# Low parts by negative copies and accumulating transfers, and a negated sine taken into a product

## The chip, the cores and the metric

The kernel runs on one core of a Trainium2 chip. The core has a matrix engine (TensorE: PE for its matmuls, PEld for its weight loads) and three engines for element-wise work (VectorE: DVE, ScalarE: ACT, GpSimd: POOL); SyncE (SP) only issues transfers. Each engine takes its instructions in the order in which they were written to its queue. Transfers (DMA) are issued from the queues of SP, ACT and POOL. The metric is the device time of one execution in microseconds.

## The reference

The input u has 2048 tokens of 448 features. It is normalised over its features (xn), and the output is the sum of three terms:

```
xn  = layernorm(u)
out = u + ssm(xn) + glu(xn)

ssm:  dt = exp(log_dt);  A = -exp(log_A_real) + i*A_imag;  C = (C_real + i*C_imag)*dt
      K[d,l] = 2 * Re( sum over n of C[d,n] * exp(A[d,n]*dt[d]*l) )      # 448 x 2048, n = 0..255
      y = causal convolution of xn with K, by an FFT of length 4096;  y + xn * D_skip
glu:  h = sigmoid(xn @ w_gate) * (xn @ w_up)       # 448 -> 1792
      h @ w_down                                    # 1792 -> 448
```

Everything is float32.

## The kernel before, in words

Two Python generators write the program, and a loop at the end of the kernel takes the next piece from the one that is further behind by its planned cost (`done`, `total`). `conv()` writes the state-space part: loads, normalisation and preparation of the parameters (`prep`), then `kgen`, which computes the kernel K in 56 chunks of 8 features, then `spectra`, which does the products in the frequency domain and the way back. `glu()` writes the gated unit. A planner that simulates the engines then sets the order of the instructions on each queue; `tc.high_priority(HP)` moves an instruction ahead in it and `tc.issue_after` holds one behind another.

**The gated unit.** The 1792 hidden features are taken as 14 tiles of 128 (`f`), in five weight groups of 3, 3, 3, 3 and 2 tiles; the tokens are taken in two halves of 1024, each in two blocks (`t`) of 512. A matmul takes float32r operands, which keep fewer bits than float32, so each operand is held as a high part (a copy rounded to float32r) and a low part (what the rounding left), and three products are summed. High and low parts are:

- weights of the gate and up projections: `wh`, `wl` (128x1024), from the loaded tile `wraw`, of which there is one buffer; `wh` is a cast on ACT (L758) and `wl` is a subtraction on DVE (L762, for f = 0 L760);
- weights of the down projection: `dh` by a cast on ACT (L788), `dl` (128x448) by a subtraction on POOL (L789), from the loaded tile `rd`;
- the gated activations of a block: `hf` (128x512, one buffer) is made on DVE from PSUM (L718); `hh` is its cast on ACT (L723), `hl` a subtraction on DVE (L725).

A call of `gate` is one tile f for one block of tokens: two series of 11 matmuls (L707), the first half for the gate and the second for the up projection. A weight step is two such calls. At the end of a weight group come the down projections (L819), four of 128 tokens for each block, each a series of three matmuls (`dh,hh`, `dl,hh`, `dh,hl`) per weight tile, summed into `acc` on DVE (L824). In the first half of the tokens all 14 weight tiles are split as told; those of the first group and of two tiles of the second are loaded and split again on POOL in the second half (L769, L770, L796), the other nine are stored to DRAM by SP (L779) and loaded from there (L774, L800).

**The chunks.** For each chunk, two matmuls give phases in PSUM (L534), ACT turns them into sines and cosines in the tile `S` (L542 to L545), DVE multiplies them with magnitudes `me` and `mf` into `Et` and `Ft` (L599 to L601), and PE takes those in 64 small matmuls (L615). The magnitudes are products on POOL (L500, L512), made for two chunks at a time with two buffers, with two squarings on ACT (L525). `S` has five slots of 512 values: sine, cosine, minus sine (half of it used), cosine, sine, with one ACT pass each for the absolute values (L542), the sines (L543), the minus sines (L544) and the cosines (L545). L599 multiplies one half of `me` with cosine and sine; L600 multiplies the other with cosine and minus sine, read backwards; L601 makes `Ft`. The phases for a pair of chunks are loaded by SP (L484).

Of the kernel before, what the change touches and what calls it, by code (L numbers as in the profile page):

```python
# [21 lines left out]
N = 256  # L22
# [4 lines left out]
TWO_PI = 2.0 * math.pi  # L27
# [8 lines left out]
HELD = 9  # L36
LATE = 3.6
# [11 lines left out]
DC = 8  # L49
# [81 lines left out]
def s4d_glu_kernel(ctx, tc, io):  # L131
# [322 lines left out]
    def kgen(pk):  # L454
# [5 lines left out]
            ("S1", [128, 5, 2 * DC, 32], F32), ("Et1", [128, 2, 2 * DC, 64], F32),  # L460
            ("Et0", [128, 2, 2 * DC, 64], F32), ("Ft", [128, 2, 2 * DC, 32], F32),
            ("S0", [128, 5, 2 * DC, 32], F32), ("mf0", [128, 4 * DC, 32], F32),
            ("me0", [128, 4 * DC, 64], F32), ("pm0", [128, 12, NCH * 2 * DC], F32),
            ("ph0", [128, 2, N], F32R), ("ph1", [128, 2, N], F32R),
        ]
        tl = {n: pk.tile(sh, dt_, name=n) for n, sh, dt_ in late}

# [59 lines left out]
        def ahead(cn):  # L527
# [13 lines left out]
            cs = S[:, 1:4:2]  # L541
            nc.scalar.activation(rows(cs), pv, AF.Abs)  # L542
            nc.scalar.activation(rows(S[:, 0:5:4]), pv, AF.Sin, scale=TWO_PI)  # L543
            nc.scalar.activation(rows(S[:, 2:3]), pv[:, :, 0:1], AF.Sin, scale=-TWO_PI)  # L544
# [34 lines left out]
        for g in range(NCK // NCH):  # L579
            for c in range(NCH):  # L580
# [19 lines left out]
                v.tensor_tensor(Et[:, :, :, 0:32], two(me[:, :, 0:32]), S[:, 1:3, :, ::-1], ALU.mult)  # L600
                fts[:] = [v.tensor_tensor(Ft, two(mf), S[:, 3:5], ALU.mult)]  # L601
# [44 lines left out]
    def rd_load(f, rd=None, eng=nc.sync):  # L646
        if rd is None:
            rd = pg.tile([128, D], F32, name="rd", bufs=RB)
        eng.dma_start(rd, io["B_w_down"][128 * f : 128 * f + 128])
        return rd  # L650

# [42 lines left out]
    def gate(w, xs, to, between=None):  # L694
# [21 lines left out]
        hf = pg.tile([128, 512], F32, name="hf", bufs=1)  # L716
# [7 lines left out]
        with hp(HP):  # L724
            v.tensor_tensor(hl, hf, hh, ALU.subtract)  # L725
        to.append((hh, hl))

    def glu():
        stores, later = [], []
        for half in range(2):  # L730
# [4 lines left out]
            for fs_ in ORDER[half]:  # L735
# [14 lines left out]
                for n_, (f, t) in enumerate(order):  # L750
                    if t == 0:
                        wh = pg.tile([128, 2, 4, 128], F32R, name="wh", bufs=2)
                        if half == 0:
# [3 lines left out]
                            with hp(HP):  # L757
                                nc.scalar.copy(wh, raw)  # L758
                                if first:
                                    v.scalar_tensor_tensor(wl, raw, lim[:, 0, 0:1], wh, ALU.mult, ALU.subtract)  # L760
                                else:
                                    v.tensor_tensor(wl, raw, wh, ALU.subtract)  # L762
# [19 lines left out]
                    if t == 0:  # L782
                        dh = pg.tile([128, D], F32R, name="dh", bufs=FCH[0])
                        if half == 0:
# [4 lines left out]
                            nc.gpsimd.tensor_tensor(dl, rd, dh, ALU.subtract)  # L789
# [244 lines left out]
    def conv():  # L1034
        with tc.tile_pool(name="psk", bufs=1, space=PSUM) as ps_, tc.tile_pool(
# [78 lines left out]
            with tc.tile_pool(name="pk", bufs=1, side="right", reuse_waits="tile") as pk:  # L1114
                yield from kgen(pk)
        yield HOLE
# [9 lines left out]
    W1s, GGs, act = [], [], []  # L1126
# [43 lines left out]
```

## Time and profile before

| | |
|---|---|
| median of 3 runs | 732.13 us (730.05 to 732.71) |
| the profiled execution | 725.02 us |
| its span, first to last instruction | 723.2 us |
| granted TensorE clock, mean | 0.984 |
| DMA | 115.72 MB, mean 160 GB/s |

A row of a group of instructions reads: line of the kernel, engine, operation, tile written <- tiles read, shapes, count | busy time in us, mean ns of one | idle time of the engine just before them, and what ended it. A row of a timeline reads: start in us, duration in us, engine, line, operation. A row of a list of stretches gives, for each engine, its busy time with the number of instructions in brackets, then the granted clock of TensorE, the share of the DMA engines and GB/s. A row of waits reads: who <- what it waited for: total us, times, longest us. A row of transfers gives the kilobytes of one and the median time from its issue to its landing, where the trace has it.

The chunks run from about 128 to 533 us.

### The profile page before, as it was taken

How to read it: one execution, taken by the hardware profiler on the slowest of the kernel's cores; microseconds unless marked ns; L12 is line 12 of the kernel's file. 1: busy time of each engine (PE TensorE's matmuls, PEld its weight loads, DVE VectorE, ACT ScalarE, POOL GpSimd, SP SyncE). 2: the span in 40 equal slices, each digit the busy share in tenths (PEclk: the TensorE clock that was granted, in tenths of full speed). 3: DMA queues.
4: the chain of work that ended last, by engine and by line, in shares of the span. 5: the costliest groups of instructions: out<-in, count | busy, mean ns of one | idle time of the engine just before them, and what ended most of it. 6: DMA issues, size and time to landing. Idle time of an engine off the chain costs nothing.

```text
span 723.2 us, 19101 instructions
## 1 busy us (share of the span) xinstructions
PE 676.3 (94%) x7780; PEld 532.4 (74%) x7780; DVE 565.1 (78%) x776; ACT 420.8 (58%) x650; POOL 384.5 (53%) x430
## 2 busy tenths in 40 slices
PE   2998799997998999998999999999999999999996
PEld 1765688786886888655778887888877787777784
DVE  5799996799989999999588988987865555565543
ACT  3646364678687788898398687776742222322320
POOL 2120027699888788789556865776855001441004
PEclk9998999999999999999999999999999999999999
DMA  9946328434414545364853232232269999999745
GB/s 205 232 111 189 94 84 266 159 107 165 151 52 135 187 136 170 106 184 140 255 159 136 61 137 97 69 111 69 74 156 250 278 235 239 247 261 238 177 128 154
DMA packets 92823, 115.72 MB, mean 160 GB/s; under 512 B 12432, under 2 KB 81200, under 8 KB 92480
## 3 DMA queue, kind: packets, MB, share of 16 engines
q1 hardware_dynamic: 83328, 94.03, 47.5%
q10 hardware_dynamic: 6704, 14.51, 6.3%
q0 software_dynamic: 2704, 5.96, 3.4%
q8 instruction: 61, 1.00, 0.6%
q14 instruction: 26, 0.21, 0.1%
HBM read 69.70 MB, written 44.76 MB: 158 GB/s over the span
## 4 chain that ended last, share of the span: by engine, by line
PE 62%; DVE 16%; ACT 8%; DMA 7%; issue 4%; SPq 2%; POOL 1%; ACTq 0%; DVEq 0%; POOLq 0%
PE gu L707 24%; PE po L819 15%; PE sp L905 7%; PE ko L615 6%; PE pv L932 4%; PE tr L534 3%; DVE Et L600 2%; DVE Ft L601 2%; DVE Et L599 2%; DVE hl L725 1%; DMA acc_d<-acc 1%; DVE pm L448 1%; ACT S L545 1%; DMA xe<-in_A_u_dram 1%; DVE wl L762 1%
## 5 line engine op out<-in xcount | busy, mean ns | idle before, releaser
L512 POOL TENSOR_TENSOR me<-me,pm 128x32 f32<-128x32 f32 (+1 forms) x168 | 146.1, 870 | 83.5 <-DVE Et L600 70.8
L512 POOL TENSOR_TENSOR mf<-mf,pm 128x64 f32<-128x64 f32 (+1 forms) x112 | 120.7, 1078 | 4.9
L707 PE MATMUL gu<-xh,wh 128*128 128x512 f32 x336 | 100.7, 406 | 1.4 <-ACT xh L220 1.4
L707 PE MATMUL gu<-xh,wl 128*128 128x512 f32 x336 | 95.4, 391 | 0.0
L707 PE MATMUL gu<-xl,wh 128*128 128x512 f32 x336 | 95.1, 390 | 0.0
L819 PE MATMUL po<-dh,hh 128*128 128x448 f32 x224 | 85.7, 383 | 6.7 <-DVE xr L224 2.6
L599 DVE TENSOR_TENSOR Et<-me,S 128x1024 f32<-128x1024 f32 x56 | 81.7, 1460 | 9.5 <-ACT S L545 7.6
L600 DVE TENSOR_TENSOR Et<-me,S 128x1024 f32<-128x1024 f32 x56 | 79.5, 1419 | 8.4 <-ACT me L525 8.4
L601 DVE TENSOR_TENSOR Ft<-mf,S 128x1024 f32<-128x1024 f32 x56 | 79.4, 1418 | 7.4 <-ACT S L545 4.4
L819 PE MATMUL po<-dl,hh 128*128 128x448 f32 x224 | 83.6, 373 | 0.0
L819 PE MATMUL po<-dh,hl 128*128 128x448 f32 x224 | 82.7, 370 | 0.0
L542 ACT ACTIVATE S<-tr 128x1024 f32<-128x1024 f32 x56 | 57.8, 1032 | 39.7 <-PE tr L534 34.8
L707 PEld LDWEIGHTS gu<-xh,wh 128*128 128x128 f32 x336 | 61.9, 192 | 20.1 <-issue 4.8
L723 ACT CAST hh<-hf 128x512 fp32r<-128x512 f32 x56 | 35.0, 626 | 70.4 <-DVE hf L718 59.4
L615 PEld LDWEIGHTS ko<-Et,Ft 128*32 128x32 f32 x3584 | 55.2, 113 | 26.5 <-issue 16.3
L707 PEld LDWEIGHTS gu<-xh,wl 128*128 128x128 f32 x336 | 62.8, 188 | 14.9 <-DVE pl L308 0.7
L707 PEld LDWEIGHTS gu<-xl,wh 128*128 128x128 f32 x336 | 63.0, 188 | 14.0 <-issue 0.7
L615 PE MATMUL ko<-Et,Ft 128*32 128x64 f32 x3584 | 65.5, 225 | 8.1 <-DVE Et L599 4.6
L718 DVE SCALAR_TENSOR_TENSOR hf<-th,gu 128x512 f32<-128x512 f32 x56 | 38.1, 680 | 37.3 <-PE gu L707 27.8
L545 ACT ACTIVATE S<-S,hpi 128x1024 f32<-128x1024 f32 x56 | 65.5, 1170 | 0.0
L824 DVE SCALAR_TENSOR_TENSOR acc<-po,acc 128x448 f32<-128x448 f32 x80 | 48.4, 615 | 20.0 <-PE po L819 19.9
L725 DVE TENSOR_TENSOR hl<-hf,hh 128x512 fp32r<-128x512 f32 x56 | 51.8, 925 | 12.5 <-ACT hh L723 12.5
(196 smaller groups left out, 1286.4 us busy)
## 6 DMA issues: line engine op xcount, KB each, us to landing
sk_d<-sk ACTq DMA_DIRECT2D x14, 512.0 KB
sx<-x_d SPq DMA_DIRECT2D x32, 224.0 KB
skl<-sk_d SPq DMA_DIRECT2D x16, 448.0 KB
vp<-v_d SPq DMA_DIRECT2D x16, 448.0 KB
v_d<-vt SPq DMA_DIRECT2D x62, 112.0 KB
wt_d<-wh SPq DMA_DIRECT2D x9, 512.0 KB
wt_d<-wl SPq DMA_DIRECT2D x9, 512.0 KB
wl<-wt_d SPq DMA_DIRECT2D x9, 512.0 KB
```

The lines of the kernel that those rows point to most:

```text
L512: ins = nc.gpsimd.tensor_tensor(m[:, :, w + a : 2 * w : n], m[:, :, a:w:n], par(base + i).unsqueeze(2).to_broadcast([128, 4 * DC, w // n]) ...
L542: nc.scalar.activation(rows(cs), pv, AF.Abs)
L545: sins[:] = [nc.scalar.activation(cs, cs, AF.Sin, scale=-TWO_PI, bias=hpi)]
L599: v.tensor_tensor(Et[:, :, :, 32:64], two(me[:, :, 32:64]), S[:, 1::-1], ALU.mult)
L600: v.tensor_tensor(Et[:, :, :, 0:32], two(me[:, :, 0:32]), S[:, 1:3, :, ::-1], ALU.mult)
L601: fts[:] = [v.tensor_tensor(Ft, two(mf), S[:, 3:5], ALU.mult)]
L615: nc.tensor.matmul(ko[32 * j : 32 * j + 32, sl], Ft[:, cc, DC * h + 4 * q + j], Et[:, cc, DC * h + 4 * q + j], start=(k == 0), stop=(k == ...
L707: glu_mm[:] = [nc.tensor.matmul(ps, a_, b_, start=(n == 0), stop=(n == len(mm) - 1))]
L725: v.tensor_tensor(hl, hf, hh, ALU.subtract)
L819: glu_mm[:] = [nc.tensor.matmul(po, a_[:, bs], w_, start=(n == 0), stop=(n == 3 * fc - 1))]
L824: v.scalar_tensor_tensor(acc[:, b], po, 0.5, acc[:, b], ALU.mult, ALU.add)
L905: mm = nc.tensor.matmul(to, tb[:kk, t, 64 * c : 64 * c + 64], rhs, start=True, stop=True, skip_group_check=True,)
```

## The change

A low part is no longer subtracted by an engine in these places. ACT writes the negative of the high part into the low part's tile, and POOL issues a transfer that adds the full value to it:

```
def low(lo, hi, full):
    nc.scalar.activation(lo, hi, AF.Identity, scale=-1.0)
    nc.gpsimd.dma_start(lo, full, accum_op=ALU.add)
```

This is done for `wl` (512 KB) and `dl` (224 KB) of the weight tiles f = 2 to 13 in the first half of the tokens, and for `hl` (256 KB) while the chunks are written (the list `hfx` is filled at the start of `kgen` and emptied at its end). In that time `hf` alternates between its buffer and a second one, `hf1`. Apart from that, `S` loses the slot of minus sines and the ACT pass that filled it, and the product of L600 is split in two: cosine by a plain product, and minus sine by a product that multiplies with -1.

```
+LOWS = 2
...
-            ("S1", [128, 5, 2 * DC, 32], F32), ("Et1", [128, 2, 2 * DC, 64], F32),
+            ("S1", [128, 4, 2 * DC, 32], F32), ("Et1", [128, 2, 2 * DC, 64], F32),
...
-            ("ph0", [128, 2, N], F32R), ("ph1", [128, 2, N], F32R),
+            ("ph0", [128, 2, N], F32R), ("ph1", [128, 2, N], F32R), ("hf1", [128, 512], F32),
         ]
         tl = {n: pk.tile(sh, dt_, name=n) for n, sh, dt_ in late}
+        hfx.append(tl["hf1"])
...
-            cs = S[:, 1:4:2]
+            cs = S[:, 1:3]
             nc.scalar.activation(rows(cs), pv, AF.Abs)
-            nc.scalar.activation(rows(S[:, 0:5:4]), pv, AF.Sin, scale=TWO_PI)
-            nc.scalar.activation(rows(S[:, 2:3]), pv[:, :, 0:1], AF.Sin, scale=-TWO_PI)
+            nc.scalar.activation(rows(S[:, 0:4:3]), pv, AF.Sin, scale=TWO_PI)
...
-                v.tensor_tensor(Et[:, :, :, 0:32], two(me[:, :, 0:32]), S[:, 1:3, :, ::-1], ALU.mult)
-                fts[:] = [v.tensor_tensor(Ft, two(mf), S[:, 3:5], ALU.mult)]
+                v.tensor_tensor(Et[:, 0, :, 0:32], me[:, :, 0:32], S[:, 1, :, ::-1], ALU.mult)
+                v.scalar_tensor_tensor(Et[:, 1, :, 0:32], me[:, :, 0:32], -1.0, S[:, 0, :, ::-1], ALU.mult, ALU.mult)
+                fts[:] = [v.tensor_tensor(Ft, two(mf), S[:, 2:4], ALU.mult)]
...
-        hf = pg.tile([128, 512], F32, name="hf", bufs=1)
+        if hfx and len(hfs) % 2:
+            hf = hfx[0]
+        else:
+            hf = pg.tile([128, 512], F32, name="hf", bufs=1)
...
-            v.tensor_tensor(hl, hf, hh, ALU.subtract)
+            if not hfx:
+                v.tensor_tensor(hl, hf, hh, ALU.subtract)
+            else:
+                low(hl, hh, hf)
...
+                                elif f < LOWS:
+                                    v.tensor_tensor(wl, raw, wh, ALU.subtract)
                                 else:
-                                    v.tensor_tensor(wl, raw, wh, ALU.subtract)
+                                    low(wl, wh, raw)
...
-                            nc.gpsimd.tensor_tensor(dl, rd, dh, ALU.subtract)
+                            if f < LOWS:
+                                nc.gpsimd.tensor_tensor(dl, rd, dh, ALU.subtract)
+                            else:
+                                low(dl, dh, rd)
...
                 yield from kgen(pk)
+                hfx.clear()
```

More of the change, by code (lines that the diff above doesn't have):

```diff
@@ L1125, in s4d_glu_kernel @@
     xq, psc, raws, acl, marks, slots, pqs = list(x_first), [], [], [], [None, None], {}, []
-    W1s, GGs, act = [], [], []
+    W1s, GGs, act, hfx = [], [], [], []
     gens = [conv(), glu()]
```

2 lines of the change are left out of this document (1 added, 1 removed).

## The prediction

> **What bounds the kernel now.** I read the share of each engine first, then the time by stage, then the chain of work that ended last inside each stage, then the groups of instructions that the change touches.
>
> ```profile
> span 723.2 us, 19101 instructions
> PE 676.3 (94%) x7780; PEld 532.4 (74%) x7780; DVE 565.1 (78%) x776; ACT 420.8 (58%) x650; POOL 384.5 (53%) x430
> ```
>
> The profiled execution took 725.02 us, 723.2 of it the span; the median of the three plain runs is 732.13 us, 1% more. Sums below are made on the profiled execution and then taken off the median. Over the whole span PE is the bound, but the mean hides the stages. In the next view each row is one stretch: busy time of PE, PEld, DVE, ACT and POOL in it.
>
> ```profile
> 28.00:128.00 100.00, 91.35 (x436) 70.96 (x435) 88.62 (x158) 51.48 (x88) 25.30 (x19) 0.95 0.58 156
> 128.00:350.00 222.00, 206.88 (x2957) 161.20 (x2959) 207.01 (x221) 174.55 (x262) 184.80 (x189) 0.98 0.44 140
> 350.00:533.00 183.00, 181.87 (x2797) 150.36 (x2787) 151.89 (x158) 133.36 (x190) 126.38 (x145) 1.00 0.39 119
> 533.00:723.00 190.00, 181.55 (x1555) 138.71 (x1553) 101.16 (x191) 48.64 (x92) 43.33 (x56) 0.99 0.87 217
> ```
>
> From 128 to 350 us (the first 30 of the 56 chunks) DVE is as busy as PE, 207 of 222 us, and PE stands idle for 15.1 us. From 350 on PE is busy 181.87 of 183 us: there is 1.1 us to win there. The change leaves the stage after 533 us alone. The chain of work, by line, for 28 to 128 and for 128 to 350 us:
>
> ```profile
> by line: PE gu L707 19.2%; PE po L819 9.1%; DMA xe<-in_A_u_dram 8.0%; issue 8.0%; DVE m L316 5.9%; DVE wl L762 4.6%; DVE pl L310 4.3%; POOL fr L396 4.0%; SPq L385 3.3%; SPq L643 2.5%; DVE hl L725 2.3%; ACT wh L758 2.1%; DVE hf L718 1.9%; AC
> by line: PE gu L707 14.6%; PE po L819 13.7%; PE ko L615 8.9%; issue 6.5%; DVE Ft L601 6.4%; DVE Et L600 6.3%; PE tr L534 4.7%; DVE Et L599 4.5%; DVE pm L448 3.9%; DVE hl L725 3.1%; ACT S L545 2.8%; ACT S L542 2.4%; ACT S L543 2.0%; DVE hf L
> ```
>
> In the second stage the DVE lines that can be seen make 6.4+6.3+4.5+3.9+3.1 = 24.2%, or 53.7 us. ACT's make 7.2%, or 16 us. No POOL line is among them. DVE work is what stands between PE and its next matmul.
>
> **The change part by part.** The groups of that stage (128 to 350 us), DVE, ACT and POOL:
>
> ```profile
> L600 DVE TENSOR_TENSOR Et<-me,S 128x1024 f32<-128x1024 f32 x30 | 44.2, 1473 | 2.5 <-ACT me L525 2.5
> L725 DVE TENSOR_TENSOR hl<-hf,hh 128x512 fp32r<-128x512 f32 x16 | 18.1, 1128 | 0.0
> L762 DVE TENSOR_TENSOR wl<-wraw,wh 128x1024 fp32r<-128x1024 f32 x7 | 9.5, 1351 | 5.2 <-ACT wh L758 5.2
> L544 ACT ACTIVATE S<-tr 128x512 f32<-128x512 f32 x30 | 18.2, 608 | 0.0
> L758 ACT CAST wh<-wraw 128x1024 fp32r<-128x1024 f32 x7 | 7.4, 1059 | 5.7 <-DMA ph<-phu_d 5.7
> L788 ACT CAST dh<-rd 128x448 fp32r<-128x448 f32 x8 | 4.6, 575 | 0.0
> L789 POOL TENSOR_TENSOR dl<-rd,dh 128x448 fp32r<-128x448 f32 x8 | 15.1, 1892 | 0.0
> ```
>
> And, over the whole span, an ACT pass of about 512 elements, POOL's issue of a transfer, the times to landing of POOL's transfers, the two spreads (min/median/max ns) that size the split product, and a two-operand DVE pair:
>
> ```profile
> L301 ACT ACTIVATE ki<-ex 112x514 int32<-112x514 f32 x2 | 1.2, 626 | 0.1
> L649 POOL DMA_DIRECT2D rdw<-in_B_w_down_dram x5 | 2.9, 573 | 1.2 <-POOL wl L770 1.2
> rdw<-in_B_w_down_dram POOLq DMA_DIRECT2D x5, 224.0 KB, 5.2
> wf<-in_c_wf_dram POOLq DMA_DIRECT2D x1, 512.0 KB, 7.1
> out_dram<-acc POOLq DMA_DIRECT2D x8, 56.0 KB, 2.9
> sel<-in_c_sel_dram POOLq DMA_DIRECT2D x1, 256.0 KB, 11.3
> L725 DVE TENSOR_TENSOR hl<-hf,hh x56: 623/692/2662, 29.8 to 691.3; 128x512 fp32r<-128x512 f32 x56
> L600 DVE TENSOR_TENSOR Et<-me,S x56: 1208/1222/2175, 139.1 to 530.4; 128x1024 f32<-128x1024 f32 x56
> L370 DVE SCALAR_TENSOR_TENSOR w<-w,s 112x512 f32<-112x512 f32 x2 | 1.4, 693 | 0.3
> L352 DVE TENSOR_TENSOR w<-a,b 112x512 f32<-112x512 f32 x2 | 1.4, 682 | 0.0
> ```
>
> *DVE, 128 to 350 us.* Sixteen hl (18.1) and seven wl (9.5) leave it: 27.6 us. The one product L600 of 1024 elements becomes two of 512. By the medians that is 2 x 692 - 1222 = 162 ns more, x30 = 4.9 us. The ends: by the minima 2 x 623 - 1208 = 38 ns, 1.1 us; by the means of this stage 2 x 1128 - 1473 = 783 ns, 23.5 us. I take the median because the means of hl hold its waits. Net relief 22.7 us of 207 (4 to 26).
>
> *ACT, same stage.* The pass L544 goes: -18.2. Negative copies come: 16 x 0.626 + 7 x 1.059 + 8 x 0.575 = 22.0. Net +3.8 on 174.6 us, with 47 us idle to take it. A copy waits for nothing but the cast just before it; behind it are the sines (L542, L545) that Et waits for.
>
> *POOL, same stage.* Eight subtractions dl go (-15.1); 16 + 7 + 8 = 31 issues at 573 ns come (+17.8). Net +2.7 on 184.8 us. What counts more is order: each issue waits for its copy on ACT, and the products of the magnitudes (L512) are queued behind it; the next chunk pair's squares on ACT and Et on DVE wait for those. Today the queue waits the other way round:
>
> ```profile
> POOL me L512 <- DVE Et L600: 70.8, 23, 11.4
> DVE Et L600 <- ACT me L525: 8.4, 12, 1.4
> ```
>
> POOL idles 70.8 us for DVE to free me, so a pause of under a microsecond for a copy is hidden there; without that idle time it would go straight into L525 and L600.
>
> *SP.* The reload of the only wraw buffer and the stores of wl and dl now wait for a landing instead of a subtraction, and the phase loads (L484) are queued behind them. wl lands 1.06 + 0.57 + 7.1 = 8.7 us after its wh, in place of about 1.4. A weight step is two gates, and 16 gates in 222 us make 28 us for one: wl has two buffers and is not wanted earlier than that, so I cost it at nothing; without that cover PE would wait 7 us at each wl. hf, too, is now held until its landing; it gets a second buffer, and gates stand 14 us apart.
>
> *How much reaches the end.* In 128 to 350 us the chain's DVE part shrinks with DVE's load: 53.7 x 22.7 / 207 = -5.9 us (ends: 0, and the whole idle time of PE, -15.1). ACT's part grows 16 x 3.8 / 174.6 = +0.4. After 350 us: 0, PE is full.
>
> *The start, 28 to 128 us.* wl is 4.6% of that chain, 4.6 us. Three wl stand in an unbroken run of DVE work:
>
> ```profile
> 44.09 1.22 DVE L762 TENSOR_TENSOR wl<-wraw,wh 128x1024 fp32r<-128x1024 f32 x1
> 61.00 1.16 DVE L762 TENSOR_TENSOR wl<-wraw,wh 128x1024 fp32r<-128x1024 f32 x1
> 73.34 1.22 DVE L762 TENSOR_TENSOR wl<-wraw,wh 128x1024 fp32r<-128x1024 f32 x1
> 107.29 1.60 POOL L789 TENSOR_TENSOR dl<-rd,dh 128x448 fp32r<-128x448 f32 x1
> ```
>
> They are worth -3.6, less what their ACT copies push back; I take -3.3 (ends 0, -4.6). The dl at 107 stands ahead of L396, which is on the chain: 1.60 becomes 0.57, -1.0.
>
> *What is late next: hl at the end of a weight group.* The first down projection reads the hl of the group's last weight step in its ninth matmul. Three such ends, the cast hh of that gate and the ninth matmul:
>
> ```profile
> 249.84 0.62 ACT L723 CAST hh<-hf 128x512 fp32r<-128x512 f32 x1 [3.09 <-DVE hf L718]
> 253.95 0.36 PE L819 MATMUL po<-dh,hl 128*128 128x448 f32 x1
> 387.58 0.62 ACT L723 CAST hh<-hf 128x512 fp32r<-128x512 f32 x1
> 396.18 0.36 PE L819 MATMUL po<-dh,hl 128*128 128x448 f32 x1
> 453.40 0.64 ACT L723 CAST hh<-hf 128x512 fp32r<-128x512 f32 x1
> 460.33 0.36 PE L819 MATMUL po<-dh,hl 128*128 128x448 f32 x1
> ```
>
> After hh come the copy (0.63), the issue (0.57) and the landing. No accumulating transfer is in the trace; nearest is rdw, 224 KB in rows of 1.8 KB, 5.2 us; the ends are 2.9 and 11.3. With 5.2, hl is there 6.4 us after hh: 256.9 (2.9 late), 394.6 (1.6 early), 460.4 (0.1 late): +3.0. With 2.9: +0.6. With 11.3: 9.0 + 4.5 + 6.2 = +19.7.
>
> The Trainium skill, page "DMA: Bandwidth & Descriptors", section "Anatomy of one DMA — SWDGE (gpsimd) path", puts such a transfer at about 2.0 us plus its bytes over 436 GB/s, an estimate of 2.6 us for hl; by it the term would be about +0.3 and the sum 2.7 us lower. The trace does not agree on the same path (5.2 for 224 KB), so the row is kept.
>
> **Sum:** -5.9 + 0.4 - 3.3 - 1.0 + 3.0 = -6.8 us: 718.2 for the profiled execution, 725.3 from the median. I say 725.
>
> **The rivals.**
>
> 1. *Slower: the landing.* The transfer reads its target as well as its source, and it shares engines with loads. For it: sel took 11.3 us for the same 256 KB. Against: sel ran in the first slices of the span, where the transfer engines are at 9 tenths; in the chunks (slices 8 to 29 of 40) they are at 2 to 8:
>
> ```profile
> DMA  9946328434414545364853232232269999999745
> ```
>  Without the hl term the sum is -9.8, so it decides where the three ends cost 9.8, at a landing of 8.0 us (5.7 + 1.2 + 2.9); at 11.3 it gives +9.9, 742.
>
> 2. *Slower: an issue held on POOL.* If the planner puts the issue behind a product that waits for Et, hl is late by that wait, 70.8 / 23 = 3.1 us in the mean. The three ends then cost 6.0 + 1.5 + 3.2 = 10.7, with -9.8 some 733; with the longest (11.4) at the first of them 14.3 + 1.5 + 3.2 = 19.0, 741. It decides from a mean of about 6 us; I count it as slower.
>
> 3. *No change: the relief does not arrive.* ACT rises to 178 of 222 us and its copies stand ahead of the sines that Et waits for. If the -5.9 and half the start go that way: 732.13 - 1.7 - 1.0 + 3.0 + 0.4 = 733.
>
> 4. *No change: the negated product runs at half speed.* The rows give 693 ns for the scalar form with two SBUF operands and 682 for the plain one, so I give it little. At half speed 512 elements cost 1208 - 623 = 585 ns more, x30 = 17.6; the relief is 5.1, its term -1.3, the time 730. The Trainium skill, page "Vector Engine (DVE) Microarchitecture Reference", section "Points that are easy to get wrong", says that this form with two non-bf16 SBUF sources halves throughput; this rival is that rule, and the trace's two rows disagree with it.
>
> 5. *Faster still: PE takes up all its idle time,* -15.1 in place of -5.9, hl hidden: 732.13 - 15.1 - 4.3 + 0.4 = 713.
>
> **How the numbers follow.** A difference of 0.5% (3.7 us) is about what this measurement can tell from none. Forecast 0.42 (own range 720 to 728), rival 5 0.14: faster 0.56. Rival 3 0.12, rival 4 0.04: same 0.16. Rival 1 0.20, rival 2 0.08: slower 0.28. The range runs from 713 (rival 5) to 742 (the longest landing in the trace).
>
> **What would show it.** Right: DVE busy about 184 us of a stage near 215, no hl or wl among its groups until the chunks end, PE idle in the stage under 12 us; the two half products near 0.69 us each; POOL's transfers into hl landing near 5 us. Wrong: PE waiting on a transfer into hl or wl by name, each beyond 3 us; POOL's me waiting for ACT's copies instead of Et; landings of 8 us and more; half products over 1 us; ACT on the chain with more than 7%.

## The result: 4% slower

| | before | after |
|---|---|---|
| median of the runs side by side | 731.09 us (4 runs, 726.04 to 732.71) | 763.45 us (4 runs, 753.98 to 767.91) |
| ratio after / before | | 1.041, 95% interval 1.030 to 1.053 |
| the profiled execution | 725.02 us | 753.98 us |
| granted TensorE clock, mean | 0.984 | 0.967 |

The ratio leaves out one disturbed run of after, so it is a little under the ratio of the medians. The forecast was 725 us with a range of 713 to 742: wrong in sign, and the time lies outside the range.

The first rows of the page of after:

```profile
span 752.2 us, 19236 instructions
PE 687.1 (91%) x7780; PEld 539.5 (72%) x7780; DVE 528.8 (70%) x785; ACT 432.1 (57%) x653; POOL 357.0 (47%) x477
```

These rows and their twins in the prediction already hold the whole difference. PE runs the same 7780 matmuls in both. Its busy time went from 676.3 to 687.1, +10.8 us, and its idle time (span less busy) from 46.9 to 65.1, +18.2; the sum is the 29.0 us between the spans. DVE was relieved as meant, by 36.3 us, and the kernel lost 29. The transfers of the software queue moved 24.18 MB (5.96 before). They did not slow the packets of the largest other queue, 94.03 MB both times: those took 47.5% of the transfer engines' 723.2 us before and 45.8% of 752.2 us after, 344 us in both. Whether transfers stood longer before their packets began isn't in these figures.

By stage. The chunks of before begin at about 128 and end at about 533 us; the later stages of after are set to about the same places of the work, so the second one, which ends where `acc_d` is stored, is 246 us long in place of 222. The end of the first is left at 128 us, where the first `Ft` is already 4.2 us late:

```profile
28.00:128.00 100.00, 86.53 (x404) 64.98 (x403) 79.83 (x145) 54.22 (x91) 17.34 (x17) 0.91 0.66 160
128.00:374.00 246.00, 223.74 (x3037) 175.15 (x3036) 189.68 (x236) 187.50 (x274) 171.02 (x226) 0.96 0.70 185
374.00:564.00 190.00, 184.12 (x2787) 151.78 (x2789) 144.63 (x166) 128.10 (x177) 119.05 (x156) 0.97 0.48 132
564.00:752.00 188.00, 178.70 (x1514) 136.59 (x1502) 97.49 (x189) 48.71 (x92) 44.12 (x57) 0.99 0.90 219
```

24 of the 29 us are lost before the first half of the tokens is stored, where the weights' low parts go by transfer too. DVE fell to 77% of that stage (189.7 of 246; 207 of 222 before), and PE's idle time rose all the same, from 15.1 to 22.3 us. The granted clock fell in each of the first three stages, 0.95 to 0.91, 0.98 to 0.96 and 1.00 to 0.97.

**What PE waits for.** Those of PE's waits over the whole span that bear on the change, before and after (who <- what for: total us, times, longest):

```profile
PE ko L615 <- DVE Et L599: 4.6, 2, 2.9
PE tr L280 <- ACT x1ab L291: 3.8, 3, 1.7
PE ko L615 <- DVE Ft L601: 3.2, 4, 1.9
```

```profile
PE tr L281 <- ACT x1c L292: 7.8, 1, 7.8
PE tr L536 <- ACT S L545: 5.8, 3, 4.6
PE ko L617 <- DVE Ft L603: 5.4, 5, 2.6
PE po L837 <- DMA hl<-hf: 4.7, 2, 3.0
PE gu L714 <- DMA wl<-wraw: 3.2, 1, 3.2
PE ko L617 <- DVE Et L600: 2.2, 1, 2.2
PE po L837 <- DMA dl<-rd: 1.5, 1, 1.5
```

New are the waits for the transfers themselves, 4.7 + 3.2 + 1.5 = 9.4 us, and two long ones for ACT: 7.8 us for a copy of the first transform (3.8 for such copies before), and 4.6 us for the sines. The waits for the products of DVE, which the change was to shorten, stay at 7.6 us against 7.8.

**The wait for ACT at 187 us.** ACT, and the matmul that waits, in the timeline of after:

```profile
183.77 1.05 ACT L656 ACTIVATE wl<-wh 128x1024 fp32r<-128x1024 f32 x1
184.73 0.61 ACT L656 ACTIVATE hl<-hh 128x512 fp32r<-128x512 f32 x1
185.25 0.56 ACT L656 ACTIVATE dl<-dh 128x448 fp32r<-128x448 f32 x1
185.72 1.01 ACT L544 ACTIVATE S<-tr 128x1024 f32<-128x1024 f32 x1
186.62 1.02 ACT L545 ACTIVATE S<-tr 128x1024 f32<-128x1024 f32 x1
187.69 1.22 PE L536 MATMUL tr<-sel,ph 128*128 128x512 f32 x2 [4.60 <-ACT S L545]
```

Three negative copies stand in a row ahead of the passes that read the phases out of PSUM. The next phase matmuls need that bank, and PE stands still for 4.6 us, about two of which are the copies. The prediction had this as rival 3.

**The wait for ACT at 81 us.** The raw weight buffer is single. First the order of events in before, then in after, with SP's wait for the whole span:

```profile
62.18 0.39 SPq L641 DMA_DIRECT2D wraw<-in_B_w_gate_dram  x1
68.99 0.89 ACT L291 COPY x1c<-tr 128x896 f32<-128x896 f32 x1
71.02 1.03 ACT L758 CAST wh<-wraw 128x1024 fp32r<-128x1024 f32 x1
```

```profile
60.50 0.86 POOL L657 DMA_DIRECT2D wl<-wraw  x1 [3.03 <-ACT wl L656]
67.50 0.39 SPq L643 DMA_DIRECT2D wraw<-in_B_w_gate_dram  x1
75.07 1.04 ACT L771 CAST wh<-wraw 128x1024 fp32r<-128x1024 f32 x1 [4.25 <-DMA wraw<-in_B_w_up_dram]
76.14 1.06 ACT L656 ACTIVATE wl<-wh 128x1024 fp32r<-128x1024 f32 x1
80.07 0.88 ACT L292 COPY x1c<-tr 128x896 f32<-128x896 f32 x1
SPq L643 <- DMA wl<-wraw: 55.8, 11, 7.9
```

In before the subtraction of `wl` ends at 61.00 + 1.16 = 62.16 us and SP reloads the buffer at 62.18. In after the transfer is issued at 60.50 and the reload at 67.50, 7.0 us later, because the transfer still reads the buffer. ACT comes to the next cast and waits 4.25 us for the load, and the copy `x1c`, for which PE waits, is behind the cast and the negative copy in ACT's order. In before `x1c` stood ahead of that cast. So two things meet here, a late load and an order that puts `x1c` behind it; r3 below takes them apart.

**The clock.** The same gap at 184 us in rows of 2 us (third number from the end: granted clock):

```profile
184.00:186.00 2.00, 0.00 (x0) 0.00 (x0) 0.14 (x1) 2.00 (x4) 0.97 (x3) 1.00 0.90 352
186.00:188.00 2.00, 0.31 (x1) 0.31 (x2) 0.00 (x0) 2.00 (x3) 2.00 (x4) 0.71 0.87 169
188.00:190.00 2.00, 2.00 (x43) 1.35 (x43) 1.24 (x2) 2.00 (x5) 2.00 (x3) 0.50 0.95 166
190.00:192.00 2.00, 2.00 (x14) 1.59 (x7) 2.00 (x4) 2.00 (x4) 1.84 (x3) 0.50 1.14 166
192.00:194.00 2.00, 2.00 (x6) 1.55 (x6) 2.00 (x2) 2.00 (x4) 1.92 (x2) 0.59 0.69 168
194.00:196.00 2.00, 2.00 (x10) 1.65 (x9) 2.00 (x3) 1.28 (x3) 1.02 (x2) 1.00 0.40 91
```

PE is idle from 183.09 to 187.69. Some 3.7 us into the gap the clock falls to half, and it stays there for 6.8 us, 6.0 of them after the work has come back. The four rows lose 2 x (0.29 + 0.50 + 0.50 + 0.41) = 3.4 us of clock, on top of the 4.6 us of the gap. Over the span the loss (1 - clock) x span is 0.016 x 723.2 = 11.6 us before and 0.033 x 752.2 = 24.8 after; the 13.2 between them are what PE's busy time shows as +10.8, some of the half-clocked time being idle. The twenty kernels below bear this out: PE's busy time, for the same 7780 matmuls, rises with (1 - clock) x span (by the table's figures, correlation 0.97 and 0.85 us for each us). How much clock a gap takes with it is not fixed: e6 below has 11.7 us more of gaps and no more busy time, x4 has 12.5 us more and 16.4 us of busy time. The fall and the return at 187 to 194 us fit what the Trainium skill states, page "TensorE: Matmul & The Clock Gate", section "Part 1: The HAM clock gate (the "warmup" mystery)": half clock after an idle window of about 3.4 us and full clock again after about as much busy time; here the clock was back after 6.8 us, two such windows, in the first of which PE was still idle for 0.9 us.

### The profile page after: what moved, and what is told of

It reads as the page before. It is cut to its first block, busy times and chain, and to the rows that moved or that the text cites. A ratio compares the mean times of both kernels' runs of the same rounds, so it can differ in the third digit from the quotient of the medians.

```text
span 752.2 us, 19236 instructions
## 1 busy us (share of the span) xinstructions
PE 687.1 (91%) x7780; PEld 539.5 (72%) x7780; DVE 528.8 (70%) x785; ACT 432.1 (57%) x653; POOL 357.0 (47%) x477
## 3 DMA queue, kind: packets, MB, share of 16 engines
q1 hardware_dynamic: 83328, 94.03, 45.8%
q0 software_dynamic: 11200, 24.18, 17.1%
## 4 chain that ended last, share of the span: by engine, by line
PE 45%; DVE 4%; ACT 2%; issue 1%; POOL 0%; POOLq 0%; DVEq 0%; ACTq 0%
PE gu L714 17%; PE po L837 10%; PE sp L923 6%; PE pv L950 4%; PE ko L617 4%; PE tr L536 2%; PE pv L985 1%; PE kp L561 1%; DVE Et L600 1%; PE kq L561 1%; DVE Ft L603 1%; DVE Et L602 1%; DVE yy L934 0%; DVE yy L936 0%; DVE pd L935 0%
## 5 line engine op out<-in xcount | busy, mean ns | idle before, releaser
L514 POOL TENSOR_TENSOR me<-me,pm 128x32 f32<-128x32 f32 (+1 forms) x168 | 131.5, 783 | 58.3 <-DVE Et L601 40.4
L714 PE MATMUL gu<-xh,wh 128*128 128x512 f32 x336 | 102.9, 412 | 5.1 <-DVE xr L225 3.2
L514 POOL TENSOR_TENSOR mf<-mf,pm 128x64 f32<-128x64 f32 (+1 forms) x112 | 104.6, 934 | 5.0
L714 PE MATMUL gu<-xh,wl 128*128 128x512 f32 x336 | 98.9, 400 | 3.2 <-DMA wl<-wraw 3.2
L714 PE MATMUL gu<-xl,wh 128*128 128x512 f32 x336 | 97.0, 395 | 0.0
L603 DVE TENSOR_TENSOR Ft<-mf,S 128x1024 f32<-128x1024 f32 x56 | 77.3, 1380 | 15.0 <-PE ko L617 8.3
L600 DVE TENSOR_TENSOR Et<-me,S 128x1024 f32<-128x1024 f32 x56 | 81.2, 1450 | 4.8 <-ACT me L527 3.5
L714 PEld LDWEIGHTS gu<-xh,wl 128*128 128x128 f32 x336 | 64.6, 193 | 17.8 <-DMA wl<-wraw 3.7
L714 PEld LDWEIGHTS gu<-xl,wh 128*128 128x128 f32 x336 | 63.8, 191 | 15.1 <-issue 1.4
L601 DVE TENSOR_TENSOR Et<-me,S 128x512 f32<-128x512 f32 x56 | 49.7, 887 | 27.9 <-ACT me L527 22.4
L722 ACT ACTIVATE th<-gu 128x512 f32<-128x512 f32 x56 | 33.4, 597 | 49.9 <-PE gu L714 49.9
```

The lines of the kernel that those rows point to most:

```text
L514: ins = nc.gpsimd.tensor_tensor(m[:, :, w + a : 2 * w : n], m[:, :, a:w:n], par(base + i).unsqueeze(2).to_broadcast([128, 4 * DC, w // n]) ...
L600: v.tensor_tensor(Et[:, :, :, 32:64], two(me[:, :, 32:64]), S[:, 1::-1], ALU.mult)
L601: v.tensor_tensor(Et[:, 0, :, 0:32], me[:, :, 0:32], S[:, 1, :, ::-1], ALU.mult)
L603: fts[:] = [v.tensor_tensor(Ft, two(mf), S[:, 2:4], ALU.mult)]
L714: glu_mm[:] = [nc.tensor.matmul(ps, a_, b_, start=(n == 0), stop=(n == len(mm) - 1))]
```

## The experiments

My theory after the result was the single raw buffer: the accumulating transfer lengthens the cycle of load, cast, negative copy, transfer and next load, and ACT, POOL and SP stand behind it. The rivals: GpSimd's queue held at the issue of `hl`; the split product; the order that the planner writes out; ScalarE's load. All kernels, with what PE did in the profiled execution (idle is span less busy; the ratios are to before, measured on the same chip):

| kernel | ratio, 95% interval | span | PE busy | PE idle | clock |
|---|---|---|---|---|---|
| before | 1 | 723.2 | 676.3 | 46.9 | 0.984 |
| after | 1.041, 1.030 to 1.053 | 752.2 | 687.1 | 65.1 | 0.967 |
| e1 sine change alone | 1.026, 1.020 to 1.032 | 741.8 | 681.1 | 60.7 | 0.979 |
| e2 sine, hl by transfer | 1.041, 1.033 to 1.049 | 755.0 | 689.1 | 65.9 | 0.965 |
| e3 sine, wl by transfer | 1.023, 1.018 to 1.028 | 746.1 | 684.1 | 62.0 | 0.974 |
| e4 sine, dl by transfer | 1.021, 1.016 to 1.026 | 743.4 | 681.4 | 62.0 | 0.973 |
| e5 sine, product whole | 1.005, 1.002 to 1.007 | 733.7 | 682.7 | 51.0 | 0.970 |
| e6 split product alone | 1.013, 1.008 to 1.018 | 734.4 | 675.8 | 58.6 | 0.980 |
| n1 two products swapped | 0.998, 0.995 to 1.000 | 725.5 | 675.3 | 50.2 | 0.988 |
| x1 no hl in the chunks | 0.999, 0.995 to 1.003 | 723.9 | 679.1 | 44.8 | 0.981 |
| x2 wl by transfer alone | 1.024, 1.020 to 1.028 | 745.7 | 687.8 | 57.9 | 0.965 |
| x6 as x2, from step 7 | 1.018, 1.009 to 1.026 | 738.0 | 683.7 | 54.3 | 0.972 |
| e8 wl and dl by transfer | 1.021, 1.015 to 1.026 | 746.0 | 687.2 | 58.8 | 0.967 |
| r3 as e8, copies on GpSimd | 1.029, 1.026 to 1.032 | 746.7 | 680.7 | 66.0 | 0.976 |
| r2 as e2, last hl subtracted | 1.034, 1.029 to 1.040 | 752.3 | 688.2 | 64.1 | 0.964 |
| x5 tanh in hf's buffer | 1.013, 1.008 to 1.018 | 737.9 | 684.7 | 53.2 | 0.969 |
| x4 as x5, hl by transfer | 1.025, 1.018 to 1.033 | 752.1 | 692.7 | 59.4 | 0.960 |
| e7 as x5, all by transfer | 1.041, 1.034 to 1.048 | 760.6 | 689.4 | 71.2 | 0.967 |
| r0 after, tanh in hf's buffer | 1.045, 1.036 to 1.055 | 763.4 | 686.7 | 76.7 | 0.968 |
| r1 as r0, second raw buffer | 1.049, 1.042 to 1.056 | 765.0 | 695.2 | 69.8 | 0.958 |

**One part at a time on top of the sine change.** e1 has the four slots and the split product and subtracts every low part; e2, e3 and e4 each put one kind of low part back to the transfer. The edit for e1, on after (with the second `hf` buffer out, too):

```diff
-            if not hfx:
-                v.tensor_tensor(hl, hf, hh, ALU.subtract)
-            else:
-                low(hl, hh, hf)
+            v.tensor_tensor(hl, hf, hh, ALU.subtract)
-                                elif f < LOWS:
+                                elif f < 99:
-                            if f < LOWS:
+                            if f < 99:
```

> Only the sine change: four slots in S and the split lower half product; all low parts by subtraction as before. Raw-buffer theory (the accumulating transfer lengthens the cycle load, high part, low part, next load of the one raw weight buffer, and ScalarE, SP and GpSimd stand behind it in order): nothing of that is here, so 727 to 735 us. Rival that the split product (one more VectorE instruction in a chunk, three alternations with GpSimd in place of two) carries the loss: 745 us or more. Third, all parts carry a share: about 735 to 742.

> The sine change and hl by transfer (second hf buffer), weights' low parts by subtraction. Raw-buffer theory: 727 to 738 us, at most the 5 us that the second half of the chunks of the changed kernel lost, and no wait of SP's queue for a wl transfer. Rival that GpSimd's queue, held at the issue of hl behind ScalarE's copy, delays the magnitudes: 745 to 755 us, most of the loss of the whole change.

> The sine change and wl by transfer alone. Raw-buffer theory: 743 to 757 us, with the loss before the first half of the tokens is stored (about 10 us or more of the changed kernel's 24), SP's reload of the raw buffer waiting for the wl transfer in the waits, ScalarE's wh cast waiting for the raw load. Rival (hl on GpSimd's queue): within 3 us of the kernel with the sine change alone.

> The sine change and dl by transfer alone. Raw-buffer theory: within 3 us of the kernel with the sine change alone, since rd has two buffers. Rival that SP's queue, held at the stores of dl behind its transfer, delays the phase loads and the raw load behind them: 740 us or more, with the wait of the store line for a dl transfer among SP's longest.

Medians: 750.2, 757.5, 747.6 and 745.2 us. The raw-buffer theory missed: the sine change, expected to be free, carries 2.6%, and `hl` adds 1.5% to it. e2 lies above the ranges of both theories. e3 lies in the raw-buffer theory's range, but within 3 us of e1, as its rival had it: `wl` adds nothing on top of the sine change. e4 lies 5 us under e1 with overlapping intervals, so `dl` adds nothing either.

**What in the sine change costs.** e5 is e1 with the product whole, the negation left out of the computation:

```diff
-                v.tensor_tensor(Et[:, 0, :, 0:32], me[:, :, 0:32], S[:, 1, :, ::-1], ALU.mult)
-                v.scalar_tensor_tensor(Et[:, 1, :, 0:32], me[:, :, 0:32], -1.0, S[:, 0, :, ::-1], ALU.mult, ALU.mult)
+                v.tensor_tensor(Et[:, :, :, 0:32], two(me[:, :, 0:32]), S[:, 1::-1, :, ::-1], ALU.mult)
```

e6 is before with nothing but the split, by the two slots that it has:

```diff
-                v.tensor_tensor(Et[:, :, :, 0:32], two(me[:, :, 0:32]), S[:, 1:3, :, ::-1], ALU.mult)
+                for i in range(2):
+                    v.tensor_tensor(Et[:, i, :, 0:32], me[:, :, 0:32], S[:, 1 + i, :, ::-1], ALU.mult)
```

> The sine change alone, but with the lower half product kept as one VectorE instruction: four slots in S, ScalarE's pass over the negated sine gone, and the negation left out of the computation (the lower half uses the positive sine). Split theory (each of the two half products takes 0.93 us in place of 0.71, the half of 1.42, so 0.44 us a chunk in a stage that VectorE binds, some 14 us over 31 chunks): the loss is gone, 722 to 733 us. Rival that the loss of the sine change comes from ScalarE's side or from the order the planner gives when the pass is missing: 742 to 750 us.

> Before, with only the lower half product in two VectorE products, by the cosine slot and by the negated sine slot as before; five slots and ScalarE's pass stay. Split theory: 742 to 750 us, as with the whole sine change, with half products of 0.9 to 1.0 us on average and 0.68 us at best. Rival (the pass or the order): 728 to 734 us. If it is the negating form of the product and not the split, 730 to 735 us.

Medians 732.9 and 739.4 us. The split is the larger part: 1.3% alone, and 2.6% falls to 0.5% when it is undone. e5 is where the split theory had it. e6 lies between the two ranges, so the split alone doesn't give the whole 2.6%; what gives the rest stays open. The half products in e6 (min/median/max ns), and what PE waited for there:

```profile
L601 DVE TENSOR_TENSOR Et<-me,S x112: 674/792/1820, 137.1 to 541.4; 128x512 f32<-128x512 f32 x112
L601 DVE TENSOR_TENSOR Et<-me,S 128x512 f32<-128x512 f32 x112 | 101.5, 924 | 17.0 <-ACT me L525 11.9 <-ACT S L544 3.8 <-POOL me L512 1.3
PE ko L616 <- DVE Ft L602: 12.5, 8, 4.4
PE ko L616 <- DVE Et L599: 7.1, 3, 3.9
```

Two halves take 2 x 0.924 = 1.85 us where the whole took 1.42. PE's waits of `ko` for DVE rose from 7.8 to 19.6 us, +11.8, and PE's whole idle time by 11.7. Its busy time didn't rise. Here the sum closes: in the profiled executions the loss is that wait.

**Is it only the order?** n1 writes the two `Et` products of before the other way round.

> Before, with the lower half product written ahead of the upper one: the same instructions, so only the order that the planner writes out can differ. If the losses of 1 to 2.6% come from the work itself: 727 to 734 us. If any new order costs that much (the kernel of before having the best of many): 738 us or more.

727.5 us; from before not to be told. The queues of this kernel are written by a planner, and a small edit moves many instructions. This new order costs nothing, but it is one order of many: x5 below, which adds no instruction, costs 1.3%, and the place of `x1c` in ACT's queue decides over 7 us. How much of the other losses is order stays open.

**Is DVE's relief worth anything?** x1 is before without the 35 subtractions of `hl` in the chunks, with nothing in their place:

```diff
-            v.tensor_tensor(hl, hf, hh, ALU.subtract)
-        to.append((hh, hl))
+            if not hfx:
+                v.tensor_tensor(hl, hf, hh, ALU.subtract)
+        to.append((hh, hh if hfx else hl))
```

> Before, with the 35 subtractions of hl in the chunks left out (the down products read hh in place of hl, so that part of the computation is wrong): VectorE is relieved of 0.93 us each and nothing is put in its place. If the prediction's relief term is right (18.1 us of VectorE's 207 in the stage are worth 18.1 / 207 x 53.7 = 4.7 us): about 725 us, 721 to 727. If relief of VectorE is worth nothing here: 728 to 733 us.

729.8 us, ratio 0.999 (0.995 to 1.003): this relief of DVE is worth nothing that can be measured, 3.5 us at the end of the interval, and the 4.7 us of the prediction's term are outside it. DVE's busy time fell from 565.1 to 537.9 us, PE's idle time only from 46.9 to 44.8. Two stretches show where it went:

```profile
128.00:250.00 122.00, 116.45 (x1636) 95.07 (x1636) 112.23 (x112) 97.92 (x142) 111.16 (x111) 1.00 0.45 148
250.00:374.00 124.00, 115.79 (x1685) 84.95 (x1684) 94.57 (x108) 92.45 (x145) 85.46 (x98) 0.94 0.52 155
```

The chunks were ahead of before by up to 12.4 us (`Ft` of the 15th chunk), still by 11.0 at the 27th, and had given it all back by the 30th, at 352 us. From 250 to 374 us DVE has 29 us to spare, and PE still stands idle for 8.2 us, against 6.6 in the same stretch of before.

**wl alone, and where.** x2 is before with `wl` by transfer from step 2 on, x6 the same from step 7 on, so without the steps ahead of the chunks; the one edit between them is

```diff
-LOWS = 2
+LOWS = 7
```

e8 has `wl` and `dl` by transfer, and r3 is e8 with the negative copies on GpSimd:

```diff
-        nc.scalar.activation(lo, hi, AF.Identity, scale=-1.0)
+        nc.gpsimd.tensor_scalar(lo, hi, -1.0, None, ALU.mult)
```

> Before, with wl alone by transfer. If the loss of wl and dl together (745.5 us) is wl's wait on TensorE (3.5 us of idle), the late first transforms at the start (+3.5) and the half clock that follows: 738 to 744 us. If it is the pair's load on ScalarE's queue, half of it each: 734 to 740. Raw-buffer theory: 742 or more.

> Before, with wl alone by transfer, and only from weight step 7 on (before with it from step 2 on: 747.4 us). If the loss of wl is TensorE's idle time from its late low parts, each with the half clock behind it, then the steps before the chunks carry the 5 us less of TensorE's work and the 3.6 us of later first transforms of the first 128 us: 735 to 741 us, with no more than one wait for wl. If the loss comes from the chunks' stage alone: 744 us or more.

> wl and dl by transfer, hl by subtraction and the sine as before. By the pair of kernels with and without them on top of the sine change (747.5 and 745.2 against 750.2 us): 726 to 732 us. Raw-buffer theory: 736 to 745 us. If VectorE's relief of 9.5 us counts where it isn't used up by the split: 720 to 727 us.

> wl and dl by transfer, hl by subtraction and the sine as before, with the negative copy on GpSimd in place of ScalarE. If the loss of that pair (745.5 us) is ScalarE's load, 99 of 122 us in the stretch from 128 to 250 against 91 before, and GpSimd's waits for its copies: 730 to 738 us. Raw-buffer theory: 743 to 750 us, since the reload still waits for the transfer.

Medians 747.4, 739.7, 745.5 and 748.9 us. `wl` alone costs 2.4%, though it adds nothing on top of the sine change, and `dl` adds nothing to it. x2 lies above the 738 to 744 that I gave to its waits, in the raw-buffer theory's open range. e8 misses my expectation of 726 to 732 and lies just above the raw-buffer theory's 736 to 745; x6 and r3 lie where their first and second ranges had them. With the copies on GpSimd, r3, it is no faster, but that doesn't clear ACT's queue: PE's wait for `x1c`, 7.3 us in e8, is 0.3 in r3, and its waits for `Ft` (13.0 against 7.0) and for `dl` (9.4 against 3.2) have grown. r3 trades one wait for others. Its `x1c` and its reload:

```profile
68.50 0.89 ACT L292 COPY x1c<-tr 128x896 f32<-128x896 f32 x1
71.10 0.39 SPq L642 DMA_DIRECT2D wraw<-in_B_w_gate_dram  x1
```

The reload comes later than in after (71.10 against 67.50), and the cast waits 5.00 us for it; but `x1c` stands ahead of the cast again, as in before, and PE doesn't wait. x5 is the reverse: it has no such transfer, `x1c` stands behind the cast, and PE waits 3.8 us for it. So by these kernels the 7 us come of a late reload together with an order that puts `x1c` behind it. PE's waits in x2, then the first 128 us of before, x2 and x6:

```profile
PE gu L713 <- DMA wl<-wraw: 9.0, 3, 3.7
PE tr L281 <- ACT x1c L292: 7.4, 1, 7.4
```

```profile
0.00:128.00 128.00, 106.05 (x490) 82.09 (x491) 105.00 (x208) 64.28 (x107) 29.99 (x41) 0.96 0.66 170
```

```profile
0.00:128.00 128.00, 101.41 (x450) 76.20 (x451) 98.03 (x197) 65.69 (x105) 27.26 (x39) 0.92 0.71 170
```

```profile
0.00:128.00 128.00, 105.14 (x482) 81.26 (x483) 107.94 (x216) 63.54 (x106) 29.86 (x41) 0.95 0.65 166
```

Ahead of the chunks x2 does 40 matmuls fewer by 128 us than before, at a lower clock, and x6 has nearly all of that back. The times agree in size, 7.7 us between the medians, but the intervals of x2 and x6 overlap, so that share is shown by the profile and not by the times; and as x6 has no long wait for `x1c`, it holds the order in ACT's queue too. In x6 two waits for `wl` were left, where I had expected one at most. Of the 22.5 us by which x2's span is longer than that of before, 11.0 are idle time (the wait for `wl` makes 9.0 more than before, those for the copies of the first transform, 7.4 + 1.0, make 4.6 more, and other waits are shorter) and 11.5 are busy time at the lower clock.

**hl.** r2 is e2 with the last `hl` of each weight group subtracted on DVE:

```diff
-            if not hfx:
+            if not hfx or last_:
```

> The sine change and hl by transfer, except for the last weight step of each group, whose hl is subtracted on VectorE. If the loss of hl (757.5 against 750.2 us) is TensorE's wait for the last hl of a group, 7.0 us in the stretch from 384 to 505 us: 746 to 752 us and no wait of the down products for hl. If it is GpSimd's queue or ScalarE's copy: 754 us or more.

x4 puts `hl` by transfer on before. For room its tanh is written into the buffer of `hf`, of which there are two; x5 is that edit alone:

```diff
-        th = pg.tile([128, 512], F32, name="th", bufs=1)
+        th = hf = pg.tile([128, 512], F32, name="hf", bufs=2)
```

> Before, with hl alone by transfer, the tanh in the buffer of hf, of which there are two. If TensorE's wait for hl at the ends of the groups and the half clock behind it make the loss (11.6 us of idle with the sine change): 738 to 748 us, with down products waiting for hl. If the transfer harms only beside the split product: 725 to 732 us.

> The control of the last: before, with the tanh in the buffer of hf, two of them, and every low part by subtraction. If this edit is harmless: 726 to 733 us. If it delays what it is meant to spare (the multiply waits for the buffer): 734 us or more, and the runs that use it are to be read against this one.

Medians 753.9, 750.9 and 739.2 us. The row that made me try r2 is that of e2,

```profile
PE po L837 <- DMA hl<-hf: 11.6, 5, 3.8
```

and in r2 there is no such wait among the eleven longest. Yet r2 got back about half of what `hl` costs at the median (753.9 against 757.5, the intervals overlap), between the two ranges given for it: its PE idles 64.1 us in place of 65.9, waiting for sines (6.7 us) and `Ft` (9.6) instead. So the wait at the group's end is not the whole cost of `hl`, and the rest stays open. x5, an edit that I had thought harmless, costs 1.3%; its PE waits 11.5 us for `Ft` where before waits 3.2, and why is open. By the ratios `hl` costs 1.2% against it (the intervals touch) and 1.5% against e1. x4 lies above both ranges given for it.

**The raw buffer, and the parts together.** r0 is after with the tanh in `hf`'s buffer, r1 the same with a second raw buffer in the chunks' pool, e7 all three transfers with the sine of before.

r1 on r0:

```diff
-            ("ph0", [128, 2, N], F32R), ("ph1", [128, 2, N], F32R),
+            ("ph0", [128, 2, N], F32R), ("ph1", [128, 2, N], F32R), ("raw2", [128, 2, 4, 128], F32),
-                                raws.append((w_load(f + 1), None))
+                                raws.append((w_load(f + 1, hfx[0] if hfx and f % 2 else None), None))
```

> The whole change, with a second raw weight buffer in the chunks' pool for every other weight step, so that the next raw load need not wait for the wl transfer; for room, tanh goes into the buffer of hf. Raw-buffer theory: the loss before the first half of the tokens is stored shrinks, 742 to 753 us against 763. If the split product and the hl landings carry the loss: 757 to 766 us, though ScalarE's waits for the raw load shrink.

> The control of the second raw buffer: the whole change with the tanh in the buffer of hf, two of them, and one raw weight buffer. If the second raw buffer is worth nothing: 760 to 770 us, as with it (766.9). If it was worth something that the in-place tanh hid (that edit alone cost 9 us on top of before): 772 us or more.

> All three low parts by transfer, the sine as before; for room, the tanh goes into the buffer of hf, of which there are two. If the two parts add up (the sine change +17 us of 24 to 32, hl +9, wl and dl nothing): 735 to 743 us. If the transfers do harm only beside the split product: 724 to 732 us, VectorE's relief then showing. If the raw-buffer theory still has something: above 745 us.

Medians 766.9, 762.7 and 763.0 us. r0 is where it was expected without any worth of the second buffer, and r1, a little above both of its ranges, is no faster. That doesn't free the queue, though. In r0 SP's reloads wait 42.1 us for `wl` to land; in r1 SP waits nearly as long, 41.4 us, most of it now at the stores of `wl` (L790), which stand in the same queue:

```profile
SPq L643 <- DMA wl<-wraw: 14.5, 4, 6.8
SPq L790 <- DMA wl<-wraw: 14.4, 2, 7.6
SPq L790 <- DMA wl<-raw: 12.5, 3, 6.9
```

So in the chunks a second raw buffer is worth nothing; whether SP's wait for the landing costs anything there, r1 can't tell. Ahead of the chunks, where r1 has no second buffer, the events at 60 to 81 us above stand. e7 was expected at 735 to 743 if the parts added up, and misses it by 20; it lies in the range above 745 that was left to the raw-buffer theory. Against r0: once all low parts go by transfer, undoing the sine change gains nothing, though alone it costs 2.6%.

**What is settled and what is open.** Settled: relief of DVE by `hl` is worth nothing that can be measured, the split costs what PE waits more for DVE, and each kind of transfer shows among PE's waits by name. Open: the rest of the sine change, the rest of `hl`, what x5 loses, and how much of each loss is the planner's order. The losses do not add: split 1.3%, `wl` 2.4%, `hl` 1.2 to 1.5%, sine 2.6%, all together 4.1%. That PE stands idle once when several things are late together would do that, but no run shows it by itself. No version was measurably faster than before.

## Why the prediction was wrong, by its steps

The sign and the size failed in different steps. With the relief (-5.9) and the start (-3.3) at nothing the sum would have been +2.4 us and the time 734.5, still inside the range. What carried it beyond are terms put at nothing or too small: the split product (e6 is 9.4 us above before) and the late landing of `wl` (x2 is 18.2 us above), and with them the half clock behind PE's gaps. The two do not add up to the whole, as said above.

- **"DVE work is what stands between PE and its next matmul"; relief of 22.7 us worth -5.9, the start -3.3.** This gave the forecast its sign. The relief came (DVE 565.1 to 528.8 us) and no gain is seen from it: x1 gives the share of `hl`, 18.1 of the 27.6 us, free of cost and stays at 0.999. No run gives that of `wl` free; in after the start came out later, not earlier. PE's waits for the products of DVE, 7.8 us over the whole span of before, were the figure to look at: -5.9 asked for most of them. I scaled the share of DVE on the chain with its load; a chain of waits tells who came last, not what comes next when that one is early. The 15.1 us of idle PE were an upper end that rival 5 took as a time.
- **The split product, 4.9 us of DVE by the medians.** Mis-sized. It measured 2 x 0.924 - 1.42 = 0.43 us a chunk in e6, 13 us over 30 chunks in place of 4.9 and 24 over all 56, and PE waited 11.8 us more for it. I had the upper end, 23.5, from the means and set it aside because "the means of hl hold its waits"; the half products' mean, 0.924, lies above their median, 0.792, too. Rival 4, the negated form at half speed, was rightly small:

```profile
L602 DVE SCALAR_TENSOR_TENSOR Et<-me,S x56: 673/694/3882, 138.7 to 555.4; 128x512 f32<-128x512 f32 x56
L601 DVE TENSOR_TENSOR Et<-me,S x56: 675/692/2901, 142.5 to 557.7; 128x512 f32<-128x512 f32 x56
```

  In after the two forms agree to 2 ns at the minimum and at the median. In e1 the minimum is 675 for both, but the median of the negated one is 800 against 692; e6, with two plain halves, has 792 over both, so that is not the form's own speed. The halving that the Trainium skill states on the page "Vector Engine (DVE) Microarchitecture Reference", section "Points that are easy to get wrong", isn't seen in these two.
- **The SP step, "I cost it at nothing", because two gates "make 28 us for one".** This step failed, and the time with it. That spacing is that of the chunks' stage; ahead of it the cast at 75.07 us follows the one before it by 17 us, it can start only when the raw load has landed, and so the 7.0 us fall on the next load. PE waits for `wl` 3.2 us in after and 9.0 in x2, and for the copy behind the cast 7.8, which r3 shows to hang on ACT's order as well. The text named the price of a lost cover, 7 us, and didn't ask where the cover is thinner, nor what stands behind the late cast.
- **ACT, +0.4.** The load was about right (in the second stage the copies took 23.7 us where 22.0 were forecast), the order was not: three copies in a row ahead of the sines, about 2 of PE's 4.6 us of waiting in one place. Rival 3 described it but priced it as relief lost, never as a loss.
- **hl at the group's end, +3.0.** About right for after, 4.7 us of waits; in e2 it was 11.6, more than the 9.8 at which rival 1 decides. But the landings were shorter than the 5.2 I took for `hl`, so it wasn't by rival 1's long landings. (The DMA row that rival 1 reads goes from 1 to 8 in slices 8 to 29, not from 2.)

```profile
hl<-hf POOLq DMA_DIRECT2D x35, 256.0 KB, 4.2
wl<-wraw POOLq DMA_DIRECT2D x12, 512.0 KB, 5.2
```

- **POOL, "hidden".** Not shown. The 70.8 us that POOL idles for DVE are those of the whole span; in the stage they are 25.4 us, in 12 waits. And POOL's issues wait long for ACT's copies,

```profile
POOL hl L657 <- ACT hl L656: 38.6, 13, 5.8
```

  3 us in the mean of those 13 waits, where I had written "under a microsecond"; those for `dl` and `wl` come to 22.4 and 20.8 us. Rival 2 had 3.1 us, but for a product that waits for `Et`. And an issue took 0.87 us at the median (L657), not the 0.573 of the sum: 31 of them make 27 us in place of 17.8. What that does to the end isn't separable in these runs.
- **hf's second buffer, nothing.** DVE waited 6.9 us for it in after:

```profile
L728 DVE SCALAR_TENSOR_TENSOR hf<-th,gu 128x512 f32<-128x512 f32 x56 | 38.2, 682 | 52.8 <-PE gu L714 32.4 <-DMA hl<-hf 6.9 <-ACT th L722 5.7
```

- **The clock was in no term.** 10.8 of the 29.0 us are PE's busy time alone. A sum over waits could at best have found 18.2.
- **The signs.** Of those named for being wrong, PE's waits for `hl` and `wl` by name came, at the bound of 3 us set for each (4.7 us in two, the longer 3.0; 3.2 in one); half products over 1 us and landings of 8 us in the median did not. Of those for being right, the two half products near 0.69 us came at the median and not in the mean (`L601` 0.887).
- **The dl at 107 us and the stage after 533 us.** `dl` costs nothing and gains nothing (e4, e8). The last stage is 190 us in before and 188 in after, near the nothing that was forecast.

## What to carry to other kernels

Where TensorE is busy for over 90% of the time, ask of each edit which of its instructions come later, and not which engine has less to do: relief of an engine that shows on the chain may be worth nothing, while a short delay on an in-order queue can hold TensorE. Price a gap in TensorE's work with the half clock behind it; here 18.2 us more of gaps came with 10.8 us more of busy time, in other kernels of the table with none or with as much again. When a subtraction becomes a transfer, follow the buffer that the transfer still reads, to its next load and to all that stands behind that load in every queue, at the place where the steps are shortest. When a planner writes the queues, compare the order around each new wait with the order of before.

## What the hardware showed that was not expected

- A gap of 4.6 us in TensorE's work was followed by about 6 us at a granted clock of 0.50 while it had work.
- VectorE products that run beside GpSimd's work are longer, the half ones by as much as the whole ones. In e1, from 128 to 374 us, the half products that overlap GpSimd instructions for less than a fifth of their time take 0.68 us in the mean (16 of 62), those that overlap for more than four fifths 0.99 (39 of 62); for the whole products of before it is 1.21 (18 of 97) and 1.45 (72 of 97). The means rise by 0.31 and 0.24 us. That GpSimd is the cause is not shown; no run takes its work away.
- An accumulating transfer of 512 KB landed in 5.2 us at the median of after and one of 256 KB in 4.2. Half the bytes save only 1.0 us.
- Writing the tanh into the buffer that the multiply then overwrites, with two of them, cost 1.3%, though it takes nothing away and adds no instruction.
